# Attention and expert layer on one core: the first block's k and q by SyncE and ScalarE in fp32, two blocks ahead of w_in

## The chip, the cores and the metric

The kernel runs on one core of one Trainium2 chip. The metric is the device time of one execution in microseconds (us); lower is better. Several runs of the kernel were timed, and one more execution was taken with the hardware profiler.

## What is computed

```python
scores = (q @ k.T) / sqrt(64)                     # batch 8, heads 8, seq 576, head_dim 64
bias   = -slope[h] * abs(i - j)                   # one slope for each head
mask   = (i - j >= 0) & (i - j < 128)             # a causal window of 128
x      = softmax(where(mask, scores + bias, -1e9)) @ v
x      = x.transpose(0, 2, 1, 3).reshape(4608, 512)
h      = x @ w_in                                 # 512 -> 2048
out    = (relu(h) ** 2) @ w_out                   # 2048 -> 512
```

All inputs and the output are fp32; the kernel computes in bf16 with fp32 sums.

## The kernel before, in words

The 4608 tokens come as 40 attention blocks (`NBLK`): each of the 8 batches has four blocks of 128 tokens and one of 64. A block needs its k, q and v for all 8 heads; with the window of 128 its scores also touch the block before it in the same batch. The steps of block `m` are written in `attention(m)`:

- `load_block` issues three loads on GpSimd's queue (POOL), for k and q into one tile `kq` (a ring of four) and for v into `vt` (a ring of six). They cast from fp32 to bf16 on the way.
- For the first ten blocks TensorE transposes k and q, 128 columns at a time (`tp`, eight matmuls against `ident`), and VectorE or ScalarE copy the result from PSUM to `kqT` ("evict"); k's half is `i = 0`, q's half `i = 1`. In the version before, the first transposes of a block ask for both k and q of it, and both copies for all eight transposes. Later blocks are transposed by a DMA that SyncE issues.
- A burst of score matmuls writes four PSUM tiles `ps_s` (ring `a`), ScalarE takes four exponentials into `P`, VectorE multiplies them with `masks` (the decay of each head, built once from `dist`, which an iota on POOL makes).
- The `pv` matmuls multiply with v, in two halves of four heads; v has a column of ones, so that the sum of the weights comes along. VectorE takes the reciprocal (`rec`) and multiplies (`x`).
- `x` is transposed into `xT`, by TensorE (`xp`) for the first blocks, by a DMA later.

The expert layer takes 512 tokens at a time (`g`, nine groups). `fc_step` multiplies `xT` with `w_in`, four matmuls for each of 16 slices of 128 columns, ScalarE applies relu (`rt`), VectorE or ScalarE square it (`g`). For the first two groups these steps are split by tokens (`SPLIT`), so that they can begin with the first block alone. The second product is done plainly for the first group (`plain`) and for the others with seven products instead of eight on halves of 256 (`product`, with sums of `g` in `S` and differences of `w_out` in `w_mix`). w_in and w_out come in four quarters each (`load_w_in`, `load_w_out`), also on POOL's queue. SyncE issues the stores of the output from `osb` (a ring of four).

The order of all this is not the program's text. Every step is a task with the engines that may run it and its estimated duration, a key (when it is due), what it depends on and which ring slots it takes. `Plan.order` runs through all tasks once, engine by engine, and always takes the task that can start first; the engine's stream is then emitted in that order, and each engine works through its own stream strictly in order. The planner's picture of the machine is a few constants: how long a result takes to reach another engine (`LAT`), when TensorE's first, slower spell ends (`COLD`), and for a load its start after the issue, its time on the DMA engines (`dma`) and its landing.

The order in which the loads are due is a line of text:

```python
FIRST = "b0 i0 b1 i1 b2 i2 b3 i3 b4 b5 b6 o0 b7 o1 b8 o2 b9 o3"
```

where `b0` is block 0's k, q and v, `i0` the first quarter of w_in and `o0` the first quarter of w_out.

Of the kernel before, what the change touches and what calls it, by code (L numbers as in the profile page):

```python
# [8 lines left out]
FP32 = mybir.dt.float32  # L9
BF16 = mybir.dt.bfloat16  # L10
# [26 lines left out]
class Plan:  # L37
# [1 line left out]

    LAT = {"PE": 260.0, "ACT": 290.0, "DVE": 270.0, "POOL": 200.0, "SP": 2200.0}  # L40
    BEGIN = {"POOL": 1250.0}
    COLD = 15000.0

    def __init__(self, bufs):
        self.tasks = []
# [11 lines left out]
    def order(self):  # L57
        used = {tag: [] for tag in self.bufs}
        free = {}
        cand = {}  # L60
        left = {}
        for t in self.tasks:
            left[t] = len(t.deps)
            for d in t.deps:
                d.users.append(t)
            for e in t.engs:
                free.setdefault(e, self.BEGIN.get(e, 800.0))
                cand.setdefault(e, [])
# [24 lines left out]
        while len(done) < n_all:  # L93
            best = None
            for e, c in cand.items():
                lo = None
                for t in c:
                    a = avail(t)
                    if a is None:
                        continue  # L100
                    st = max(a, free[e])
                    k = (st, t.key, t.seq)
                    if lo is None or k < lo[0]:
                        lo = (k, t)
                if lo is not None and (best is None or lo[0][0] < best[0]):
                    best = (lo[0][0], e, lo[1])
            if best is None:
                raise RuntimeError("plan is stuck: " + repr([
                    (e, t.key, [s.tag for s in t.acq if avail(t) is None]) for e, c in cand.items() for t in c
                    if e != "POOL"][:40]))  # L110
            st, e, t = best
            t.eng, t.start = e, st
            dur = t.engs[e] * (2 if e == "PE" and st < self.COLD else 1)
            if t.dma is not None:
                at = max(st + dur + 900.0, self.dma_free)
                self.dma_free = at + t.dma
                t.end = self.dma_free + 900.0
            else:
                t.end = st + dur + (self.LAT[e] if t.lat is None else t.lat)
            free[e] = st + dur  # L120
            for x in t.engs:
                cand[x].remove(t)
            for s in t.acq:
                if s.idx is not None:
                    continue
                s.idx = len(used[s.tag]) % self.bufs[s.tag]
                used[s.tag].append(s)
            for s in t.rel:
# [14 lines left out]
def kernel(  # L143
# [15 lines left out]
    NG = NT // 512  # L159
    NBLK = B * NKB  # L160

    FIRST = "b0 i0 b1 i1 b2 i2 b3 i3 b4 b5 b6 o0 b7 o1 b8 o2 b9 o3"
    SPLIT = ([(0, 128), (128, 256), (256, 384), (384, 512)], [(0, 256), (256, 512)])

    KQ_DMA, X_DMA = 10, 13
# [36 lines left out]
    def mm(n):  # L202
        return max(n, 64) / 2.4 + 1.5
# [75 lines left out]
    def load_block(m, key):  # L279
        b, kb = divmod(m, NKB)  # L280
        n = blk[kb]
        s_in[m, "k"] = s_in[m, "q"] = Slot("kq")
        s_in[m, "v"] = Slot("v")
        for i, (nm, src) in enumerate((("k", k), ("q", q), ("v", v))):
            sl = s_in[m, nm]

            def emit(i=i, src=src, sl=sl, nm=nm):
                o = (vt[sl.idx][0:n, :, 0:D] if nm == "v"
                     else kq[sl.idx][0:n, i].rearrange("s (h d) -> s h d", h=H))
                nc.gpsimd.dma_start(o, src[b, :, kb * 128:kb * 128 + n, :].rearrange("h s d -> s h d"))  # L290
            t_in[m, nm] = load(key + 0.01 * i, 1050.0 * n / 128, emit, [t_ones] if nm == "v" else [], [sl])
# [10 lines left out]
    def copy(task, o, i):  # L302
        if task.eng == "DVE":
            nc.vector.tensor_copy(o, i)  # L304
        else:
            nc.scalar.activation(o, i, AF.Copy)  # L306

    def attention(m):
# [14 lines left out]
                             [s_in[m, "k"]], dma=1400.0)]  # L323
        else:
            slot = Slot("h" if first else "a")
            last = None
            for i in range(2 * C):
                def emit(i=i):
                    if i == 0:
                        slot.tile = psum.tile([128, 1024], BF16, tag=slot.tag, bufs=plan.bufs[slot.tag], name="tp")  # L330
                    nc.tensor.transpose(slot.tile[:, i * 128:(i + 1) * 128],  # L331
                                        kq[s_in[m, "k"].idx][:, i // C, (i % C) * 128:(i % C + 1) * 128], ident)
                last = plan.add({"PE": mm(128)}, due - 56, emit,
                                [last, t_ident, t_in[m, "kq"[i // C]]] + ([t_in[m, "q"]] + chain["tp"] if i == 0 else []),
                                [slot, sk] if i == 0 else [], [s_in[m, "k"]] if i == 2 * C - 1 else [])
            chain["tp"] = [last]
            t_kq = []
            for i in range(2):
                def evac(i=i):
                    copy(t_kq[i], kqT[sk.idx][:, i * C:(i + 1) * C, 0:n],  # L340
                         slot.tile[:, i * 512:(i + 1) * 512].rearrange("p (c s) -> p c s", c=C)[:, :, 0:n])
                t_kq.append(plan.add(both if first else {("DVE", "ACT")[i]: both[("DVE", "ACT")[i]]},
                                     due - 56, evac, [last], [], [slot]))
        t_kq_of[m] = t_kq


# [348 lines left out]
```

## Time and profile before

| | |
|---|---|
| median of 3 runs | 308.45 us (308.12 to 308.74) |
| the profiled execution | 308.27 us |
| its span from first to last instruction | 306.1 us |
| TensorE (PE) busy | 289.8 us, 95% of the span |
| VectorE (DVE) busy | 212.2 us |
| ScalarE (ACT) busy | 200.0 us |
| GpSimd (POOL) busy | 107.6 us |
| loads issued by POOL | 18.36 MB in 116736 packets |
| moved by hardware queues | 20.46 MB in 54128 packets |

The span is what the profile's rows cover; the execution's own time is 2.2 us longer. Durations of single instructions come from this one execution, so sums are made against its 308.27 us, which lies 0.18 us below the median. Names on the left of an arrow are written, names on the right are read; L12 is line 12 of the kernel; x4 after a row means that four equal instructions are merged in it; the bracket at the end of a timeline row says how long the engine had been idle before it and what ended that. "Landing" is the time from a load's issue to the arrival of its last byte.

### The profile page before, as it was taken

Reading aid. Unit: us, or ns where it says so; the run is one execution under the profiler, and the core shown is the slowest. Engines: PE = TensorE matmul, PEld = TensorE weight load, DVE = VectorE, ACT = ScalarE, POOL = GpSimd, SP = SyncE. Lnnn points to the kernel's source line nnn. Section 1 sums busy time; section 2 is a strip of 40 time slices with the busy share of each in tenths; the row PEclk is TensorE's granted clock in tenths of the full one; section 3 lists DMA queues with packets and bytes.
Section 4 is the critical chain, followed back from the end, with each engine's and each line's share of the span. In section 5 each row is a group of like instructions: output and inputs, shape, how many; then the busy total and the mean of one; then the engine's idle time right before and its main releaser. Section 6 shows DMA issues by size and latency. Waiting matters only on the chain.

```text
span 306.1 us, 7855 instructions
## 1 busy us (share of the span) xinstructions
PE 289.8 (95%) x3076; PEld 205.9 (67%) x3076; DVE 212.2 (69%) x633; ACT 200.0 (65%) x395; POOL 107.6 (35%) x133
## 2 busy tenths in 40 slices
PE   1489999999999999999999999999999999999995
PEld 1279987686866677666666666666766676666783
DVE  4348888749968786678758776677677785545622
ACT  4178894759769666767767787777667785564410
POOL 8747938626265444226361327132200000000000
PEclk9999999999999999999999999999999999999999
DMA  8999999999999999999999999999884112201223
GB/s 60 179 175 166 151 189 173 130 184 139 151 151 144 164 157 169 155 154 182 165 153 166 156 139 149 130 165 146 139 55 120 30 42 62 69 0 36 69 72 103
DMA packets 170901, 39.31 MB, mean 128 GB/s; under 512 B 158064, under 2 KB 170352, under 8 KB 170864
## 3 DMA queue, kind: packets, MB, share of 16 engines
q0 software_dynamic: 116736, 18.36, 93.9%
q1 hardware_dynamic: 54128, 20.46, 41.3%
q8 instruction: 24, 0.39, 0.5%
q14 instruction: 13, 0.11, 0.1%
HBM read 36.70 MB, written 9.44 MB: 151 GB/s over the span
## 4 chain that ended last, share of the span: by engine, by line
PE 92%; DMA 3%; DVE 2%; POOL 2%; ACT 1%; issue 0%; POOLq 0%; DVEq 0%
PE h L477 42%; PE o L559 32%; PE ps_s L361 6%; PE pv L397 6%; PE o L628 4%; DMA kq<-in_q_dram 3%; PE tp L331 1%; POOL kq L290 1%; PE xp L442 1%; ACT kqT L306 1%; DVE w_mix L273 0%; DVE kqT L304 0%; POOL vt L290 0%; DVE osb L593 0%; POOL w_in_sb L256 0%
## 5 line engine op out<-in xcount | busy, mean ns | idle before, releaser
L477 PE MATMUL h<-xT,w_in_sb 128*128 128x512 bf16 (+2 forms) x832 | 150.8, 316 | 0.3 <-DVE x L423 0.3
L487 ACT ACTIVATE rt<-h 128x512 bf16<-128x512 f32 x144 | 86.0, 600 | 61.9 <-PE h L477 54.2
L477 PEld LDWEIGHTS <-w_in_sb 128*128 128x128 bf16 x832 | 71.0, 99 | 35.4 <-DVE x L423 0.8
L374 ACT ACTIVATE P<-ps_s 128x512 bf16<-128x512 f32 (+1 forms) x160 | 71.1, 520 | 9.7 <-PE ps_s L361 9.5
L495 DVE TENSOR_TENSOR g<-rt 128x512 bf16<-128x512 bf16 x91 | 38.3, 422 | 35.1 <-ACT rt L487 34.4
L382 DVE TENSOR_TENSOR P<-P,masks 128x512 bf16<-128x512 bf16 (+1 forms) x160 | 54.4, 364 | 8.0 <-ACT P L374 6.5
L559 PEld LDWEIGHTS <-g 128*128 128x128 bf16 x512 | 47.9, 98 | 15.1
L290 POOL DMA_DIRECT2D kq<-in_k_dram x40 | 34.2, 855 | 55.6 <-DMA kqT<-kq 48.4
L290 POOL DMA_DIRECT2D vt<-in_v_dram x40 | 34.1, 856 | 52.8 <-PE pv L397 46.6
L559 PEld LDWEIGHTS <-S 128*128 128x128 bf16 x384 | 35.8, 98 | 11.7 <-issue 0.7
L559 PE MATMUL o<-w_mix,S 128*128 128x256 bf16 x256 | 38.7, 273 | 0.0
L559 PE MATMUL o<-w_mix,g 128*128 128x256 bf16 x256 | 37.5, 273 | 0.0
L559 PE MATMUL o<-w_out_sb,g 128*128 128x256 bf16 x256 | 36.9, 273 | 0.0
L290 POOL DMA_DIRECT2D kq<-in_q_dram x40 | 34.3, 857 | 2.0 <-DMA kq<-in_k_dram 1.3
L497 ACT ACTIVATE g<-rt 128x512 bf16<-128x512 bf16 x53 | 33.5, 632 | 1.3
L423 DVE TENSOR_TENSOR x<-pv,rec 128x256 bf16<-128x256 f32 (+1 forms) x80 | 33.3, 417 | 1.1
L397 PEld LDWEIGHTS <-P 128*128 128x128 bf16 x576 | 27.3, 98 | 8.9 <-DVE P L382 1.2
L397 PE MATMUL pv<-vt,P 128*128 128x65 bf16 x576 | 31.5, 194 | 0.6 <-DVE P L382 0.6
L418 DVE RECIPROCAL rec<-pv 128x4 f32<-128x4 f32 (+1 forms) x80 | 14.2, 177 | 14.6 <-PE pv L397 14.2
L361 PEld LDWEIGHTS <-kqT 64*128 64x128 bf16 x576 | 15.7, 96 | 11.1 <-issue 8.9
L361 PE MATMUL ps_s<-kqT 64*128 64x128 bf16 (+1 forms) x320 | 20.1, 216 | 0.8 <-DVE kqT L304 0.8
L361 PE MATMUL ps_s<-kqT,kqT 64*128 64x128 bf16 (+1 forms) x256 | 17.0, 214 | 1.4 <-ACT kqT L306 1.4
(41 smaller groups left out, 190.6 us busy)
## 6 DMA issues: line engine op xcount, KB each, us to landing
out_dram<-osb SPq DMA_DIRECT2D x35, 256.0 KB, 4.3
kq<-in_k_dram POOLq DMA_DIRECT2D x32, 128.0 KB, 7.1
kq<-in_q_dram POOLq DMA_DIRECT2D x32, 128.0 KB, 7.4
vt<-in_v_dram POOLq DMA_DIRECT2D x32, 128.0 KB, 8.2
w_in_sb<-in_moe_w_in_dram POOLq DMA_DIRECT2D x4, 512.0 KB, 9.8
w_out_sb<-in_moe_w_out_dram POOLq DMA_DIRECT2D x4, 512.0 KB, 10.0
kq<-in_k_dram POOLq DMA_DIRECT2D x8, 64.0 KB, 9.2
kq<-in_q_dram POOLq DMA_DIRECT2D x8, 64.0 KB, 8.9
```

The source lines that it names most:

```text
L290: nc.gpsimd.dma_start(o, src[b, :, kb * 128:kb * 128 + n, :].rearrange("h s d -> s h d"))
L361: nc.tensor.matmul(slot_s[2 * (c // 2) + half].tile.rearrange("p (c t q) -> p c t q", c=2, t=2)[:, c % 2, part, 0:n], kqT[sk_of[mk].idx][r ...
L374: nc.scalar.activation(view(Pt[sP.idx][:, 2 * i:2 * i + 2]), view(slot_s[i].tile.rearrange("p (c t q) -> p c t q", c=2, t=2)), AF.Exp, bia ...
L382: nc.vector.tensor_tensor(pt, pt, view(masks[:, 2 * i:2 * i + 2]), op=ALU.mult)
L397: nc.tensor.matmul(slot_v.tile[:, hi * (D + 1):(hi + 1) * (D + 1)], Pt[sP.idx][:, place(h), part, :], vt[s_in[mk, "v"].idx][:, h, :], star ...
L418: nc.vector.reciprocal(srec.tile[0:n, :], pv[0:n, :, D])
L423: nc.vector.tensor_tensor(xt[sx.idx][0:n, hf * 256:(hf + 1) * 256].rearrange("p (h e) -> p h e", h=4), pv[0:n, :, 0:D], srec.tile[0:n, :]. ...
L477: nc.tensor.matmul(slot.tile[:, f * w:(f + 1) * w], w_in_sb[:, cc, (fc + f) * 128:(fc + f + 1) * 128], xT[:, cc, g * 512 + lo:g * 512 + hi ...
L487: nc.scalar.activation(srt.tile, slot.tile, AF.Relu, bias=0.0, scale=1.0)
L495: nc.vector.tensor_tensor(o, i, i, op=ALU.mult)
L497: nc.scalar.activation(o, i, AF.Square)
L559: nc.tensor.matmul(bank.tile[:, t * 256:(t + 1) * 256], left(g, what, j)[:, t * 128:(t + 1) * 128], right(by, j), start=opens and j == 0 a ...
```

## The change

Five edits go together. Block 0's k and q are no longer loaded and cast by POOL: SyncE loads k and ScalarE loads q as fp32 into two `osb` tiles, and VectorE casts each into `kq`. Block 1's loads move ahead of the first quarter of w_in, and the third quarter of w_in behind block 3. The iota moves to the front of POOL's queue. The transposes of k and of q become two chains: k's need only k, q's only q, and each copy to `kqT` follows its own four transposes; for block 0 both copies are VectorE's. And three constants of the planner change: TensorE's slow spell ends at 12 us instead of 15 and costs wide matmuls 1.4 instead of 2 times their duration, and loads that start in that spell take 1.2 times their time on the DMA engines and land 0.4 us later than assumed before. The constants add no instruction; they enter into the order that the planner makes for the whole kernel.

```diff
-    COLD = 15000.0
+    COLD = 12000.0
...
-            dur = t.engs[e] * (2 if e == "PE" and st < self.COLD else 1)
+            dur = t.engs[e] * (1 if e != "PE" or st > self.COLD else 2 if t.engs[e] < 250 else 1.4)
             if t.dma is not None:
-                at = max(st + dur + 900.0, self.dma_free)
-                self.dma_free = at + t.dma
-                t.end = self.dma_free + 900.0
+                early = st < self.COLD
+                at = max(st + dur + (700.0 if early else 900.0), self.dma_free)
+                self.dma_free = at + t.dma * (1.2 if early else 1.0)
+                t.end = self.dma_free + (1300.0 if early else 900.0)
...
-    FIRST = "b0 i0 b1 i1 b2 i2 b3 i3 b4 b5 b6 o0 b7 o1 b8 o2 b9 o3"
+    FIRST = "b0 b1 i0 b2 i1 b3 i2 i3 b4 b5 b6 o0 b7 o1 b8 o2 b9 o3"
...
-    t_iota = plan.add({"POOL": 360.0}, -9e5 + 0.012, build_iota)
+    t_iota = plan.add({"POOL": 360.0}, -9e5 - 1, build_iota)
...
+            if m == 0 and nm != "v":
+                st = Slot("osb")
+
+                def raw(src=src, st=st, nm=nm):
+                    st.tile = work.tile([128, 512], FP32, tag="osb", bufs=plan.bufs["osb"], name="raw")
+                    (nc.sync if nm == "k" else nc.scalar).dma_start(
+                        st.tile.rearrange("s (h d) -> s h d", h=H), src[b, :, 0:n, :].rearrange("h s d -> s h d"))
+
+                def cast(i=i, st=st, sl=sl):
+                    nc.vector.tensor_copy(kq[sl.idx][:, i], st.tile)
+                t_raw = plan.add({"SP" if nm == "k" else "ACT": 450.0}, -2e6, raw, [], [st], dma=1050.0)
+                t_in[m, nm] = plan.add({"DVE": 470.0}, key + 0.01 * i, cast, [t_raw], [sl], [st])
+                continue
...
-            for i in range(2 * C):
...
-                                [last, t_ident, t_in[m, "kq"[i // C]]] + ([t_in[m, "q"]] + chain["tp"] if i == 0 else []),
...
-            chain["tp"] = [last]
             t_kq = []
-            for i in range(2):
...
+            for j, nm in enumerate("kq"):
+                last = None
+                for i in range(C):
...
+                    last = plan.add({"PE": mm(128)}, due - 56, emit,
+                                    [last, t_ident, t_in[m, nm]] + (chain["tp"] if i == 0 else []),
+                                    [slot, sk] if i == 0 and j == 0 else [], [s_in[m, nm]] if j == 1 and i == C - 1 else [])
+                chain["tp"] = [last]
+
+                def evac(j=j):
...
+                t_kq.append(plan.add({"DVE": both["DVE"]} if m == 0 else both if first else
+                                     {("DVE", "ACT")[j]: both[("DVE", "ACT")[j]]}, due - 56, evac, [last], [], [slot]))
```

More of the change, by code (lines that the diff above doesn't have):

```diff
@@ L325, in attention @@
             slot = Slot("h" if first else "a")
-            last = None
-            for i in range(2 * C):
[L328 to L333, printed above, removed]
-                                [last, t_ident, t_in[m, "kq"[i // C]]] + ([t_in[m, "q"]] + chain["tp"] if i == 0 else []),
-                                [slot, sk] if i == 0 else [], [s_in[m, "k"]] if i == 2 * C - 1 else [])
@@ L336, in attention @@
-            chain["tp"] = [last]
-            t_kq = []
-            for i in range(2):
[L339 to L343, printed above, removed]
+            t_kq = []
@@ new lines, in attention, with emit @@
+            for j, nm in enumerate("kq"):
+                last = None
+                for i in range(C):
+                    def emit(i=i, j=j, nm=nm):
+                        if i == 0 and j == 0:
+                            slot.tile = psum.tile([128, 1024], BF16, tag=slot.tag, bufs=plan.bufs[slot.tag], name="tp")
+                        nc.tensor.transpose(slot.tile[:, (j * C + i) * 128:(j * C + i + 1) * 128],
+                                            kq[s_in[m, nm].idx][:, j, i * 128:(i + 1) * 128], ident)
+                    last = plan.add({"PE": mm(128)}, due - 56, emit,
[3 more added lines that the diff above has]
+                def evac(j=j):
+                    copy(t_kq[j], kqT[sk.idx][:, j * C:(j + 1) * C, 0:n],
+                         slot.tile[:, j * 512:(j + 1) * 512].rearrange("p (c s) -> p c s", c=C)[:, :, 0:n])
+                t_kq.append(plan.add({"DVE": both["DVE"]} if m == 0 else both if first else
+                                     {("DVE", "ACT")[j]: both[("DVE", "ACT")[j]]}, due - 56, evac, [last], [], [slot]))
```

## The prediction, made before the changed kernel ran

> **What bounds the kernel now.** I read the page first, then the windows of the first 50 us, the timeline of that stretch, the transfers with their times to landing, and the waits.
>
> ```profile
> span 306.1 us, 7855 instructions
> ...
> PE 289.8 (95%) x3076; PEld 205.9 (67%) x3076; DVE 212.2 (69%) x633; ACT 200.0 (65%) x395; POOL 107.6 (35%) x133
> ...
> PE   1489999999999999999999999999999999999995
> ...
> DMA  8999999999999999999999999999884112201223
> ...
> PE 92%; DMA 3%; DVE 2%; POOL 2%; ACT 1%; issue 0%; POOLq 0%; DVEq 0%
> ```
>
> TensorE is busy for 289.8 of 306.1 us and holds 92% of the chain that ended last. The change neither adds nor removes a matmul (3076 before and after, counted in the order of both built programs), so it can move the end only through TensorE's empty time, 16.3 us, and through how long its first matmuls run slowly. The tenths show where the empty time lies: in the first slices. The windows say how much (columns: stretch, length, busy time and instructions of PE, PEld, DVE, ACT, POOL, clock, DMA share, GB/s).
>
> ```profile
> 0.00:5.09 5.09, 0.00 (x0) 0.00 (x0) 2.56 (x13) 1.28 (x1) 3.97 (x9) 1.00 0.61 39
> 5.09:10.15 5.06, 2.92 (x24) 1.70 (x24) 2.48 (x9) 3.77 (x12) 5.06 (x7) 1.00 1.35 140
> 10.15:13.38 3.23, 0.00 (x0) 0.00 (x1) 0.66 (x3) 0.00 (x0) 1.78 (x3) 1.00 2.08 170
> 13.38:15.97 2.59, 1.65 (x13) 1.22 (x13) 0.85 (x2) 0.60 (x1) 2.19 (x4) 1.00 1.62 187
> 15.97:20.00 4.03, 4.03 (x48) 3.83 (x48) 1.70 (x4) 2.66 (x5) 2.27 (x4) 1.00 1.78 185
> 20.00:25.00 5.00, 4.28 (x89) 3.93 (x86) 3.65 (x13) 4.22 (x8) 2.57 (x4) 1.00 1.84 181
> 30.00:50.00 20.00, 20.00 (x342) 16.86 (x340) 17.67 (x61) 15.94 (x35) 13.89 (x18) 1.00 1.69 171
> 50.00:60.00 10.00, 9.66 (x132) 6.58 (x130) 7.80 (x28) 7.85 (x17) 7.13 (x10) 1.00 2.19 140
> 60.00:287.00 227.00, 227.00 (x2213) 153.96 (x2212) 163.69 (x481) 156.96 (x304) 65.06 (x78) 1.00 1.35 126
> ```
>
> Up to 15.97 us TensorE has 5.09 + 2.14 + 3.23 + 0.94 = 11.4 us of nothing to do; from there to 287 us it lacks 0.72 + 0.34 us. POOL, which issues every load, is busy for the whole of 5.09 to 10.15: the loads are issued as fast as it can. What ends TensorE's waits:
>
> ```profile
> 1.25 1.02 POOL L290 DMA_DIRECT2D kq<-in_k_dram  x1 [0.80 <-POOLq L679]
> 2.26 0.89 POOL L290 DMA_DIRECT2D kq<-in_q_dram  x1
> 3.53 1.02 POOL L290 DMA_DIRECT2D vt<-in_v_dram  x1
> 4.55 0.76 POOL L256 DMA_DIRECT2D w_in_sb<-in_moe_w_in_dram  x1
> 5.09 0.60 PE L331 MATMUL tp<-ident,kq 128*128 128x128 bf16 x4 [5.09 <-DMA kq<-in_k_dram]
> ...
> 6.35 0.61 PE L331 MATMUL tp<-ident,kq 128*128 128x128 bf16 x4 [0.65 <-DMA kq<-in_q_dram]
> ...
> 7.03 0.91 POOL L290 DMA_DIRECT2D vt<-in_v_dram  x1
> ...
> 7.80 0.61 PE L361 MATMUL ps_s<-kqT 64*128 64x128 bf16 x8 [0.85 <-DVE kqT L304]
> ...
> 10.42 0.42 DVE L423 TENSOR_TENSOR x<-pv,rec 128x256 bf16<-128x256 f32 x1
> 13.38 0.61 PE L331 MATMUL tp<-ident,kq 128*128 128x128 bf16 x4 [3.23 <-DMA kq<-in_k_dram]
> ...
> 14.62 0.63 PE L442 MATMUL xp<-ident,x 128*128 128x128 bf16 x4
> 15.29 0.42 DVE L304 COPY xT<-xp 128x512 bf16<-128x512 bf16 x1
> ...
> 16.93 3.24 PE L477 MATMUL h<-xT,w_in_sb 128*128 128x128 bf16 x32
> ```
>
> Block 0's k arrives at 5.09 and its attention ends with x at 10.84. Then TensorE has nothing until block 1's k lands at 13.38, since w_in's first quarter was issued ahead of it (4.55). Its transposes and scores follow, and the first w_in matmuls, 32 of block 0, start at 16.93. When did that first quarter land?
>
> ```profile
> w_in_sb<-in_moe_w_in_dram POOLq DMA_DIRECT2D x1, 512.0 KB, 7.9
> vt<-in_v_dram POOLq DMA_DIRECT2D x1, 128.0 KB, 8.1
> vt<-in_v_dram POOLq DMA_DIRECT2D x1, 128.0 KB, 4.7
> ```
>
> These are single issues: block 0's v takes 4.7 us from 3.53 (lands 8.23), w_in's first quarter 7.9 from 4.55 (12.45), block 1's v 8.1 from 7.03 (15.13). So w_in sat unused from 12.45 to 16.93.
>
> **The change, part by part.** The order of the changed program on POOL is: the distances, k1, v0, q1, v1, w_in's first quarter, block 2, second quarter, block 3, third and fourth quarter. k0 and q0 leave it for SP and ACT.
>
> *When w_in can start.* Before, the seven transfers k0, q0, v0, w_in, k1, q1, v1 were down at 15.13. After, the same seven must be down when w_in is, as it is last. If the transfers are the limit and starting on three queues gives nothing, it lands at 15.13. If all that POOL sheds is gained, k0's and q0's issues (1.02 + 0.89 = 1.91), it lands at 13.2. I take 13.8, nearer the second end, because POOL was the busy party (5.06 of 5.06) while the bytes ran at 140 GB/s, under the 171 of 30 to 50 us. [...]
>
> *Is block 0 ready by then?* The raw loads are in no row. Nearest are SP's own transfers, with fp32 on both sides:
>
> ```profile
> out_dram<-osb SPq DMA_DIRECT2D x35, 256.0 KB, 4.3
> out_dram<-osb SPq DMA_DIRECT2D x2, 128.0 KB, 1.7
> ```
>
> At 1.7 to 4.3 us from an issue at about 0.8 (ACT's first instruction starts at 0.74) k0 and q0 land between 2.5 and 5.1; if the two, of 256 KB each, go one after the other at 4.3 us, the second lands at 9.4. I take 5.1. A cast is a 128x512 copy: 0.42 us in the bf16 row at 15.29, and as an upper end 0.69, the fp32 row below. VectorE's distances, ahead of the casts, come 1.4 us earlier, since the iota goes first on POOL. The casts then end near 5.9, q's transposes (0.61) near 6.6, two copies (0.42 each) near 7.5, and scores start about 7.6: where they start now, 7.80. So block 0 gains nothing, and its x (10.84) plus transposes and copy (0.63 + 0.42) is done near 12, 1.8 us before 13.8. That slack is what hides the casts: raw loads up to 6.9 cost nothing, later ones one for one. k evicted without q's transposes only moves work into this slack; that VectorE takes both copies of block 0 is what it did before.
>
> ```profile
> 20.01 0.38 PE L397 MATMUL pv<-vt,P 128*128 128x65 bf16 x7
> ...
> 21.98 0.23 PE L361 MATMUL ps_s<-kqT,kqT 64*128 64x128 bf16 x2 [0.71 <-ACT kqT L306]
> 22.39 2.06 ACT L374 ACTIVATE P<-ps_s 128x512 bf16<-128x512 f32 x4
> 22.76 1.28 PE L477 MATMUL h<-xT,w_in_sb 128*128 128x128 bf16 x20
> 23.88 0.59 PE L397 MATMUL pv<-vt,P 128*128 128x65 bf16 x8
> ...
> 298.70 0.69 DVE L607 TENSOR_TENSOR osb<-o,x 128x512 f32<-128x512 f32 x1 [1.06 <-PE o L559]
> ```
>
> *Gain at the start.* At 13.8 instead of 16.93: 3.1 us. Ahead of it the new order has also done 8 of block 1's 16 pv matmuls, which before came at 20.01 (0.38 for 7): 0.4. Together 3.5.
>
> *What is late next.* The new order puts block 2's pv only 16 w_in matmuls behind its scores; before there were 4 transposes and 20. Before, pv (23.88) came 1.9 us after the scores began (21.98) and waited for nothing; the exponentials start 0.4 after the scores and take 0.52 each. Scores (0.4, until the exponentials start) and 16 matmuls (0.064 each by the 20 in 1.28: 1.0) cover 1.4 of 1.9: some 0.5 us of waiting. Block 1's x transposes stand 7 matmuls behind the end of its pv, where a reciprocal and a multiply (0.42, the row at 10.42) must run with their hand-overs: 0.5 more. I take 1.0, bounds 0.4 and 1.6. The scores' wait for ScalarE's copy of q (0.71) is in both. The second quarter should not stop TensorE: it follows block 2's three loads, 0.9 MB at the 171 GB/s of 30 to 50 us, 5.4 us after the first, near 19.2; the new order has 76 matmuls ahead of it, 4.9 us at 0.064 each, 1.3 more while the first 32 run at 0.10 (3.24 for 32) and the 1.0 of waits. [...]
>
> *The rest.* The changed constants make no instruction; they give a new order to 250 us of work. Before, TensorE waited 0.34 us between 30 and 287. The new order has tighter places. Between the scores of blocks 20 and 21 stood 28 products of 256 columns and 8 pv matmuls, now 7 and 8; between those of 15 and 16 stood 11 products, 8 w_in matmuls and 16 pv, now 13 products and 16 pv. A burst of scores needs all four score tiles back, which the exponentials of the burst before it hold for up to 2.06 us, longer where an eviction stands ahead of them. I take 1.0 us of new waits in all, bounds 0 and 3.0 (four such places with 0.75 each).
>
> Sum: 3.5 - 1.0 - 1.0 = 1.5 us less. The profiled execution took 308.27 with a span of 306.1; 2.2 lies around it. That gives 304.6 and 306.8, and against the median of the runs (308.45, 0.18 more) 306.9.
>
> **The rivals.** *More of it is kept:* w_in at 13.2 (+0.6), no new waits after 30 us (+1.0): 305.3. For it: before's long stretch without waits. Against: the tighter bursts.
>
> *The DMA engines are the limit:* w_in at 15.13, 1.3 later: 308.2, no change. For it: 170 to 187 GB/s from 10 us on. Against: the full POOL row.
>
> *The casts hold POOL up:* they run at about 5.1 to 5.9, while POOL issues v1 and w_in; if POOL stands still for both (0.84), w_in lands that much later: 307.8. For it: the issue beside VectorE's first fp32 work takes 1.02 (3.53), the ones at 2.26 and 7.03 take 0.89 and 0.91. Against: the one at 1.25 takes 1.02 as well. [...]
>
> *Slower, raw loads late:* k0 and q0 come as 2048 pieces of 256 bytes (64 fp32 for each token and head) beside POOL's loads. If the second lands at 9.4, block 0's x is transposed 2.5 after 13.8, so 306.9 + 2.5: 309.4. It turns into a loss from a landing at 8.4 (6.9 + 1.5). Against: 1.7 us for a store on an empty queue.
>
> *Slower, the order:* new waits of 3.0 instead of 1.0 give 308.9; it loses from 2.5 on.
>
> **How the numbers follow.** A measurement of this kernel tells about 0.2%, 0.6 us. The forecast (306.2 to 307.7) has 0.34, the gain kept 0.22, the DMA limit 0.10, the casts 0.08, raw loads late 0.10, the order 0.16. Faster is the first two and half of the casts (307.8 lies on the bound), 0.60; the same is the other half and the DMA limit, 0.14; slower the last two, 0.26. The range for 8 in 10 runs from 304.8 (w_in at 13.2, no late waits, and 0.5 less of the early ones: 306.9 - 2.1) to 309.2, between the two slower cases.
>
> **What would show it.** Right: the first w_in matmul at 13.2 to 14.4, released by w_in's load; scores of block 0 at 7 to 8; a wait of about 0.5 at block 2's pv; TensorE's empty time up to there 2 to 3 us less, and 0.5 to 1.5 us more between 30 and 287. Wrong: casts after 7 us, w_in after 15, or more than 2.5 us of waits after 30.

## The result, and the profile after

The changed kernel takes 305.62 us (median of 20 runs, 305.31 to 307.90), the kernel before, in the same set of runs, 307.78 (20 runs, 306.79 to 308.95): a ratio of 0.9928, 95% interval 0.9915 to 0.9942, 2.2 us less. The forecast was 1.5 less. It stood on the median of the first three runs of the kernel before, 308.45, which lies 0.7 above that of the 20. The profiled execution took 305.56, with a span of 303.8 against 306.1. Two executions of the runs below, 311.66 and 310.08, had a granted clock of 0.994 and took over 1.5% longer than the fastest of their kernel; the ratios leave them out.

The page of the changed kernel: the span and the busy times.

```profile
span 303.8 us, 7860 instructions
...
PE 290.9 (96%) x3076; PEld 205.6 (68%) x3076; DVE 216.4 (71%) x639; ACT 197.6 (65%) x391; POOL 105.8 (35%) x131
```

TensorE's busy time is 1.1 us longer than before and the span 2.3 shorter, so 3.4 us of empty time went. The windows, at the same cuts as before (columns as in the prediction), say where:

```profile
0.00:5.09 5.09, 0.00 (x0) 0.00 (x0) 2.78 (x13) 2.39 (x5) 4.28 (x10) 1.00 0.81 125
5.09:10.15 5.06, 3.31 (x28) 2.26 (x28) 3.15 (x9) 2.66 (x9) 5.06 (x7) 1.00 1.85 171
10.15:13.38 3.23, 2.67 (x35) 1.82 (x35) 2.65 (x10) 2.06 (x4) 2.81 (x5) 1.00 2.14 165
13.38:15.97 2.59, 2.59 (x32) 2.56 (x30) 1.55 (x6) 0.00 (x0) 1.84 (x3) 1.00 1.46 196
15.97:20.00 4.03, 3.24 (x60) 2.73 (x59) 2.83 (x7) 3.46 (x7) 2.25 (x3) 1.00 1.87 182
20.00:25.00 5.00, 4.67 (x92) 4.29 (x90) 4.25 (x13) 3.81 (x8) 1.96 (x3) 1.00 1.63 187
30.00:50.00 20.00, 19.78 (x290) 15.31 (x286) 17.79 (x59) 15.30 (x34) 11.92 (x16) 1.00 1.74 175
50.00:60.00 10.00, 9.62 (x121) 7.02 (x119) 6.13 (x19) 7.67 (x17) 6.12 (x7) 1.00 1.92 148
60.00:287.00 227.00, 226.89 (x2224) 153.37 (x2221) 166.12 (x486) 155.78 (x302) 65.01 (x78) 1.00 1.27 123
```

Up to 15.97 us TensorE has 5.09 + 1.75 + 0.56 = 7.4 us of nothing to do, 4.0 less than before (11.4). From 15.97 to 25 it has 0.79 + 0.33 where it had 0.72, and from 30 to 287 it has 0.22 + 0.38 + 0.11 = 0.71 where it had 0.34. The transfers moved 125 GB/s in the first 5 us instead of 39, and 171 instead of 140 in the next 5. The start, from the timeline:

```profile
0.74 0.48 ACTq L292 DMA_DIRECT2D raw<-in_q_dram  x1
0.75 0.44 SPq L292 DMA_DIRECT2D raw<-in_k_dram  x1
...
4.98 0.92 POOL L257 DMA_DIRECT2D w_in_sb<-in_moe_w_in_dram  x1
5.17 0.95 DVE L296 CAST kq<-raw 128x512 bf16<-128x512 f32 x2 [1.22 <-DMA raw<-in_q_dram]
...
6.18 0.93 PE L347 MATMUL tp<-ident,kq 128*128 128x128 bf16 x7 [6.18 <-DVE kq L296]
...
7.62 0.69 PE L347 MATMUL tp<-ident,kq 128*128 128x128 bf16 x5 [0.52 <-DVE kqT L318]
...
8.40 0.61 PE L376 MATMUL ps_s<-kqT 64*128 64x128 bf16 x8
...
12.62 0.85 PE L412 MATMUL pv<-vt,P 128*128 128x65 bf16 x8
12.81 0.41 DVE L318 COPY xT<-xp 128x512 bf16<-128x512 bf16 x1
...
13.28 1.57 PE L492 MATMUL h<-xT,w_in_sb 128*128 128x128 bf16 x13
```

and the times from issue to landing of three of these loads:

```profile
raw<-in_q_dram ACTq DMA_DIRECT2D x1, 256.0 KB, 4.4
raw<-in_k_dram SPq DMA_DIRECT2D x1, 256.0 KB, 3.9
...
w_in_sb<-in_moe_w_in_dram POOLq DMA_DIRECT2D x1, 512.0 KB, 7.0
```

k is down at 0.75 + 3.9 = 4.65, q at 0.74 + 4.4 = 5.14. VectorE's first cast waits until q is there, since q's cast stands ahead of k's; TensorE starts at 6.18, block 0's scores at 8.40 (7.80 before), and x of block 0 is in `xT` at 13.22. w_in's first quarter is down at 4.98 + 7.0 = 11.98. The first w_in matmul starts at 13.28, with no idle time ahead of it that ends with a load: it follows block 0's own chain (its copy to `xT` ends at 13.22) and, directly ahead of it on TensorE, the eight pv matmuls of block 1 from 12.62, which stand behind block 0's `xp` there. w_in had waited for 1.3 us. It lands only 0.5 us earlier than before (12.45); what comes much earlier are block 1's k, down at 1.36 + 4.9 = 6.26 instead of 13.29, and its q, at 3.25 + 4.7 = 7.95 instead of 14.17, so that TensorE's wait of 3.23 us for that k is gone. The chain that ended last says the same. Its only load in the first 16 us (start, duration):

```profile
0.74 4.40 DMA raw<-in_q_dram
...
5.17 0.96 DVE kq L296 x2
...
13.46 1.39 PE h L492 x13
```

In the same view of the kernel before the one load of the start is block 1's q, not w_in either:

```profile
6.17 8.00 DMA kq<-in_q_dram
```

What TensorE waited for over the span:

```profile
PE tp L347 <- DVE kq L296: 6.2, 1, 6.2
PE tp L347 <- DVE kqT L318: 0.9, 2, 0.5
PE xp L457 <- DVE x L438: 0.5, 1, 0.5
...
PE xp L457 <- ACT rt L502: 0.4, 1, 0.4
```

### The profile page after: what moved, and what is told of

It is laid out like the page before. It is cut to its first block, busy times and chain, and to the rows that moved or that the text cites. A ratio compares the mean times of both kernels' runs of the same rounds, so it can differ in the third digit from the quotient of the medians.

```text
span 303.8 us, 7860 instructions
## 1 busy us (share of the span) xinstructions
PE 290.9 (96%) x3076; PEld 205.6 (68%) x3076; DVE 216.4 (71%) x639; ACT 197.6 (65%) x391; POOL 105.8 (35%) x131
## 4 chain that ended last, share of the span: by engine, by line
PE 93%; DVE 3%; DMA 1%; ACT 1%; issue 0%; DVEq 0%; ACTq 0%
PE h L492 41%; PE o L574 32%; PE pv L412 6%; PE ps_s L376 6%; PE o L643 5%; PE tp L347 2%; DMA raw<-in_q_dram 1%; PE xp L457 1%; ACT P L389 1%; DVE x L438 0%; DVE S L538 0%; ACT rt L502 0%; DVE kqT L318 0%; DVE P L397 0%; DVE kq L296 0%
## 5 line engine op out<-in xcount | busy, mean ns | idle before, releaser
L492 PEld LDWEIGHTS <-w_in_sb 128*128 128x128 bf16 x832 | 69.9, 99 | 35.2
L304 POOL DMA_DIRECT2D kq<-in_k_dram x39 | 33.3, 854 | 23.9 <-DMA kqT<-kq 17.5
L304 POOL DMA_DIRECT2D kq<-in_q_dram x39 | 33.4, 855 | 4.3 <-DMA w_in_sb<-in_moe_w_in_dram 1.9
L412 PE MATMUL pv<-vt,P 128*128 128x65 bf16 x576 | 32.4, 195 | 1.0 <-DVE x L438 0.3
L433 DVE RECIPROCAL rec<-pv 128x4 f32<-128x4 f32 (+1 forms) x80 | 14.0, 176 | 13.3 <-PE pv L412 13.0
L574 PE MATMUL o<-w_out_sb,S 128*128 128x256 bf16 x128 | 17.7, 273 | 0.5 <-DVE osb L608 0.5
```

Of the source, the lines that this page charges most:

```text
L412: nc.tensor.matmul(slot_v.tile[:, hi * (D + 1):(hi + 1) * (D + 1)], Pt[sP.idx][:, place(h), part, :], vt[s_in[mk, "v"].idx][:, h, :], star ...
L492: nc.tensor.matmul(slot.tile[:, f * w:(f + 1) * w], w_in_sb[:, cc, (fc + f) * 128:(fc + f + 1) * 128], xT[:, cc, g * 512 + lo:g * 512 + hi ...
L574: nc.tensor.matmul(bank.tile[:, t * 256:(t + 1) * 256], left(g, what, j)[:, t * 128:(t + 1) * 128], right(by, j), start=opens and j == 0 a ...
```

## The experiments

**What was in question.** Theory A: block 0's chain (raw load of q, two casts, transposes, scores, `xT`) sets the first w_in matmul, and w_in's load has time to spare. The rival is the prediction's step: w_in's load sets it, and block 0 has 1.8 us to spare. A second question is which part of the edit brings the gain: the two extra queues, the order of POOL's loads, or the planner's constants. The place of the iota and the split of the transposes were not taken out alone. All kernels but two (`old_const`, `const_only`) keep the changed kernel's order on TensorE, VectorE and ScalarE, except for the one step named; the planned order is edited after the planner has made it. Each set of runs had its own runs of the kernel before: medians 307.78, 308.37, 307.83, 308.50 and 308.33.

**q's raw load later** (`late_raw`): ScalarE issues it behind the first of its eight masks.

```diff
+    late = next(t for t in done if t.eng == "ACT")
+    done.remove(late)
+    done.insert(done.index(t_mask[0]) + 1, late)
```

> The changed kernel with one instruction moved: ScalarE issues q's raw load behind its first mask, near 4.3 us instead of 0.74, so that it lands near 8.5 instead of 5.14. Theory A (block 0's chain is the bound): all of the 3.3 us is lost, scores of block 0 near 11.7, 308.9 in all. Theory B (the prediction: raw loads cost nothing up to 6.9, later ones one for one): 1.6 us lost, 307.2.

310.53 us (6 runs, 309.78 to 311.18), ratio 1.0067 (1.0045 to 1.0088). From its timeline:

```profile
3.98 0.42 ACTq L292 DMA_DIRECT2D raw<-in_q_dram  x1
...
9.38 1.78 DVE L296 CAST kq<-raw 128x512 bf16<-128x512 f32 x2 [5.43 <-DMA raw<-in_q_dram]
...
11.21 0.93 PE L347 MATMUL tp<-ident,kq 128*128 128x128 bf16 x7 [11.21 <-DVE kq L296]
```

q lands at 9.38, 4.24 later than in the changed kernel, and the two casts take 1.78 instead of 0.95. The first transposes come 5.03 later than in the changed kernel (11.21 against 6.18) and the profiled execution ends 4.87 later (310.43 against 305.56). Nearly all of it arrives at the end: block 0 has no slack, and w_in's load, which was not touched, doesn't matter here. The end is 1.6 us later than theory A gave (308.9), since q landed 0.9 later than it assumed and the casts took longer.

**w_in later** (`w_in_late`): POOL issues its first quarter behind block 2's k and q.

```diff
+    pool = [t for t in done if t.eng == "POOL"]
+    spots = [n for n, t in enumerate(done) if t.eng == "POOL"]
+    at = pool.index(t_win[0])
+    pool.insert(at + 2, pool.pop(at))
+    for n, t in zip(spots, pool):
+        done[n] = t
```

> The changed kernel with the order of every engine kept, except that on POOL's queue the first quarter of w_in is issued behind block 2's k and q instead of ahead of them. It landed at 11.98 us and the first w_in matmul started at 13.28; with two block loads (0.85 us each) ahead it should land near 13.7. Theory A (block 0's own chain, from raw loads to x, sets the first w_in matmul, and w_in has 1.3 us to spare): the first w_in matmul at about 13.8 and 0.5 us lost, 306.1 against 305.6. Theory B (the prediction: w_in's landing sets it): the matmul moves with the load, 1.7 us lost, 307.3.

307.12 us (13 runs, 305.63 to 307.61), ratio 0.9963 (0.9949 to 0.9976). The profiled execution was the fastest of them, 305.63: its w_in is down at 13.23, and the first w_in matmul at 13.36, as theory A has it. That left the other runs unexplained, so it ran again.

> The kernel with w_in's first quarter issued behind block 2's k and q, once more, since its profiled execution (305.63) was the fastest of its runs and the typical one (307.12) is 1.5 us slower than the changed kernel. Theory A (block 0's chain sets the first w_in matmul; a later w_in costs only what goes beyond 13.3) then needs another place where the typical execution loses 1 to 1.5 us: a slow spell that ends later (18 to 20 us instead of 15.8), at equal landings. Rival (the step of the prediction: w_in's landing sets it): w_in lands 1 us later than in the first profile, 14.2 to 14.6, and the first w_in matmul with it. A profile at 305.6 again, with medians at 307, leaves it open.

306.48 us (8 runs, 305.85 to 307.40), ratio 0.9955 (0.9937 to 0.9974); profiled 306.81. The landing of w_in and then the first w_in matmul in the first profile (issue at 6.83), and the same two in the second (issue at 6.92):

```profile
w_in_sb<-in_moe_w_in_dram POOLq DMA_DIRECT2D x1, 512.0 KB, 6.4
```

```profile
13.36 1.57 PE L492 MATMUL h<-xT,w_in_sb 128*128 128x128 bf16 x13
```

```profile
w_in_sb<-in_moe_w_in_dram POOLq DMA_DIRECT2D x1, 512.0 KB, 7.5
```

```profile
14.46 1.57 PE L492 MATMUL h<-xT,w_in_sb 128*128 128x128 bf16 x13 [0.82 <-DMA w_in_sb<-in_moe_w_in_dram]
```

With the same program w_in took 6.4 us in one execution and 7.5 in the other. At 13.23 it is no wait. At 6.92 + 7.5 = 14.42 it is: TensorE stands for 0.82 us, the first w_in matmul comes 1.10 later and the execution ends 1.18 later. So the step of the prediction is right in kind once w_in lands after 13.3, as the medians suggest that it does here in most runs; in the changed kernel's profiles it lands earlier.

**The changed kernel again** (`after_again`).

> The changed kernel once more, unchanged, for a comparison within one set of runs with the three others. 305.6 us as before (305.3 to 306.2), ratio to the kernel before 0.992 to 0.995. First w_in matmul at 13.3, released by block 0's chain and not by w_in's load (12.0). If a second profile shows a first w_in matmul over 0.5 us away from that, single profiles of these kernels can't tell half a microsecond, and the readings of the start have to be widened by that.

305.64 us (5 runs, 305.39 to 305.82), ratio 0.9923 (0.9905 to 0.9941). The landing of w_in:

```profile
w_in_sb<-in_moe_w_in_dram POOLq DMA_DIRECT2D x1, 512.0 KB, 7.7
```

w_in is down at 4.97 + 7.7 = 12.67, 0.7 later than in the first profile; the first w_in matmul starts 0.23 later (13.51), since block 0's first cast took 0.81 us instead of 0.43 and its transposes started 0.22 later (6.40), and the profiled times differ by 0.08 (305.64 and 305.56). w_in's landing may move by 0.7 us without a trace in the time.

**Without the two queues** (`pool_k0q0`): POOL loads and casts k0 and q0 at the head of its queue; no raw loads and no casts on VectorE, all else in the changed order. The iota, in the changed kernel ahead of the first load (0.84), comes behind these two here (3.23).

```diff
-                    st.tile = work.tile([128, 512], FP32, tag="osb", bufs=plan.bufs["osb"], name="raw")
-                    (nc.sync if nm == "k" else nc.scalar).dma_start(
-                        st.tile.rearrange("s (h d) -> s h d", h=H), src[b, :, 0:n, :].rearrange("h s d -> s h d"))
+                    nc.gpsimd.dma_start(kq[sl.idx][:, i].rearrange("s (h d) -> s h d", h=H),
+                                        src[b, :, 0:n, :].rearrange("h s d -> s h d"))
...
-                    nc.vector.tensor_copy(kq[sl.idx][:, i], st.tile)
+                    pass
```

> The changed kernel in its order, but block 0's k and q come as before: cast on the way by POOL, at the head of its queue (no raw loads, no casts on VectorE). It asks what the two hardware queues bring alone. Theory A: k0 and q0 land near 5.1 and 6.3, so block 0's transposes start no later, but all of POOL's other loads move back by 1.9 us: w_in near 13.9, k1 near 8.2, first w_in matmul at 14.2, 0.9 to 1.2 us lost, 306.6. Rival 1 (nearly all of the gain comes from the queues): 307.8, the time of the kernel before. Rival 2 (the casts eat what the queues bring): 305.6.

308.25 us (12 runs, 306.98 to 310.69), ratio 0.9998 (0.9974 to 1.0021): the whole gain goes. From its timeline:

```profile
7.13 0.79 POOL L257 DMA_DIRECT2D w_in_sb<-in_moe_w_in_dram  x1
...
10.33 0.61 PE L346 MATMUL tp<-ident,kq 128*128 128x128 bf16 x4 [1.57 <-DMA kq<-in_q_dram]
...
14.55 1.57 PE L491 MATMUL h<-xT,w_in_sb 128*128 128x128 bf16 x13
```

w_in is issued 2.15 later (7.13 against 4.98) and block 1's q is there at 10.33, for which TensorE stands 1.57 us; the first w_in matmul comes 1.27 later than in the changed kernel. That profiled execution (309.29) also has one wait of 1.5 us further on, for a transposing DMA, so the 1.27 alone don't account for its time. The fastest run, 306.98, is about what the 1.27 would give (theory A said 306.6); why the typical one loses 1.3 more is not shown. Without the two extra queues, then, nothing of the gain is left in the median, but only half of that loss is seen at the start.

**w_in back ahead of block 1** (`w_in_first`), the rest of the edit as in `w_in_late`:

```diff
-    pool.insert(at + 2, pool.pop(at))
+    pool.insert(at - 4, pool.pop(at))
```

> The changed kernel in its order, but on POOL's queue the first quarter of w_in goes back ahead of k1, v0, q1, v1. It asks what the changed order of loads brings alone. Theory A: k1 and q1 land 2.4 us later (near 8.7 and 10.4), block 0's scores stand behind k1's transposes and start near 9.9 instead of 8.40, block 1's near 11.8; the first w_in matmul, though w_in is down by 9, waits for block 0's x until 14.8: 1.5 us lost, 307.1. Theory B (w_in's landing sets the first w_in matmul): no loss, 305.6 or less.

308.61 us (12 runs, 308.15 to 308.78), ratio 1.0007 (0.9994 to 1.0020): the whole gain goes here too.

```profile
10.25 0.61 PE L347 MATMUL tp<-ident,kq 128*128 128x128 bf16 x4 [2.11 <-DMA kq<-in_k_dram]
...
16.19 1.57 PE L492 MATMUL h<-xT,w_in_sb 128*128 128x128 bf16 x13
```

w_in is issued at 1.36 and is early, but TensorE now stands 2.11 us for block 1's k, and the first w_in matmul comes 2.91 later than in the changed kernel, as does the end (308.47 against 305.56 in the profiled executions). Theory A had named this path and put the loss at 1.5. An early w_in is worth nothing when the blocks that it pushes back feed TensorE first. With either the queues or the order taken back the median gain is gone.

**The hardware queues take block 1's k and q** (`hw_k1q1`), POOL those of block 0, and behind them the iota (3.23).

```diff
+                    nc.gpsimd.dma_start(kq[sl.idx][:, i].rearrange("s (h d) -> s h d", h=H),
+                                        src[b, :, 0:n, :].rearrange("h s d -> s h d"))
...
-                        st.tile.rearrange("s (h d) -> s h d", h=H), src[b, :, 0:n, :].rearrange("h s d -> s h d"))
+                        st.tile.rearrange("s (h d) -> s h d", h=H), src[b, :, 128:256, :].rearrange("h s d -> s h d"))
...
-                    nc.vector.tensor_copy(kq[sl.idx][:, i], st.tile)
+                    nc.vector.tensor_copy(kq[s_in[1, nm].idx][:, i], st.tile)
...
+                if m == 1 and nm != "v":
+                    return
```

> SyncE and ScalarE load block 1's k and q in fp32, VectorE casts those, and POOL loads and casts block 0's k and q at the head of its queue; the same number of loads on each queue and the same order on every engine. Theory A (block 0's chain sets the first w_in matmul): k0 down at 4.9 and q0 at 6.2 (as with POOL loading all six), no cast ahead of them; scores of block 0 at 7.8 instead of 8.4, x 0.6 earlier, first w_in matmul at 12.7, 305.0. Rival (what matters is that POOL gets w_in out early, and the first bytes are shared by all queues): q0 lands at 7 or later, scores at 8.4 or later, 305.6 or slower.

305.87 us (6 runs, 305.44 to 311.66), ratio 0.9928 (0.9909 to 0.9946): no gain over the changed kernel. PEld rows are TensorE's weight loads.

```profile
5.73 0.34 PEld L351 LDWEIGHTS <-kq 128*128 128x128 bf16 x4 [5.73 <-DMA kq<-in_k_dram]
...
8.27 0.61 PE L380 MATMUL ps_s<-kqT 64*128 64x128 bf16 x8
...
13.48 0.67 PEld L496 LDWEIGHTS <-w_in_sb 128*128 128x128 bf16 x7 [0.31 <-DMA w_in_sb<-in_moe_w_in_dram]
```

The scores come at 8.27, not at 7.8 (k0 takes until 5.73), 0.13 earlier than in the changed kernel, and yet the first w_in matmul starts at 13.48: w_in was issued at 5.41 and took 8.0 us, so that it is down at 13.41, and the weight load of its first matmul waits 0.31 us for it. What block 0 wins, w_in takes back. The two limits lie within 1.5 us of each other.

**The planner's old constants under the change** (`old_const`):

```diff
-    COLD = 12000.0
+    COLD = 15000.0
...
-                at = max(st + dur + (700.0 if early else 900.0), self.dma_free)
-                self.dma_free = at + t.dma * (1.2 if early else 1.0)
-                t.end = self.dma_free + (1300.0 if early else 900.0)
+                at = max(st + dur + 900.0, self.dma_free)
+                self.dma_free = at + t.dma
+                t.end = self.dma_free + 900.0
```

> The changed kernel with the planner's three constants of the kernel before; loads, casts and their order on POOL are the change's, the order of TensorE's work differs: the transposes of block 2's k and q stand ahead of the first w_in matmuls. Theory A: block 2's k lands at 12.8 and its q a microsecond later, so the first w_in matmul comes at 14.7 instead of 13.3, with 8 transposes (0.6) already done: 0.8 slower at the start; with later waits like those of the changed kernel 306.4. Rival (the new order's tight places after 30 us are what the constants brought, 1.0 us): the old constants give that back, 305.4 or less.

306.52 us (7 runs, 306.05 to 306.99), ratio 0.9951 (0.9930 to 0.9972), 0.9 slower than the changed kernel, as theory A expected (306.4), though it had the first w_in matmul at 14.7. TensorE's order now has block 2's transposes ahead:

```profile
13.40 0.61 PE L346 MATMUL tp<-ident,kq 128*128 128x128 bf16 x4 [1.08 <-DMA kq<-in_k_dram]
...
15.53 0.62 PE L491 MATMUL h<-xT,w_in_sb 128*128 128x128 bf16 x4
```

It stands 1.08 us for block 2's k, and the first w_in matmul is at 15.53. The new constants tell the planner that early loads come later, and so keep that wait out.

**The new constants alone** (`const_only`): the same lines the other way round, on the kernel before.

> The kernel before with the three new constants of the planner alone: loads, casts and their order on POOL as before; the order of the rest is another. Theory A (the gain is in the loads and in block 0's own chain): the start is as before, first w_in matmul at 16.5 to 17.2, and the time 307.8 to 308.5, no difference. Rival (the constants bring tight places, the prediction's term of 1.0 for later waits): TensorE waits 1.0 more between 30 and 287 and the kernel is slower by as much. A gain of 0.9 as in the changed kernel (whose time rises by that with the old constants) would say that they help by themselves.

308.62 us (12 runs, 307.70 to 310.54), ratio 1.0015 (0.9996 to 1.0035): no difference, as theory A has it in the time. Its start is not as expected: block 1's k lands at 12.16 in its profile, not at 13.38, though POOL's order is that of before, and the first w_in matmul comes at 15.71 (16.93 before). With POOL's loads in the same order, part of that may be a difference between executions: w_in's first quarter takes 6.7 us from 4.54 here, and 7.9 from 4.55 in the profile of the kernel before. That gains nothing in the end. The constants are worth 0.9 us with the new loads and nothing without.

**The casts exchanged** (`k_cast_first`): k's ahead of q's, since k lands first and TensorE transposes it first.

```diff
+    qc, kc = t_in[0, "q"], t_in[0, "k"]
+    n, i = done.index(qc), done.index(kc)
+    done[n], done[i] = kc, qc
```

> The changed kernel with the two casts of block 0 exchanged on VectorE: k's first, then q's. In the changed kernel q's stands first, so k, down at 4.65, waits for q, down at 5.14, and TensorE's first transposes (of k) for both casts. Theory A (block 0's chain sets the first w_in matmul): first transposes at 5.2 to 5.3 instead of 6.2 to 6.4, scores of block 0 at 7.4 instead of 8.4 to 8.6, x's transposes 1.1 earlier; the first w_in matmul then comes when both that chain (12.2) and w_in (12.0 to 12.7 in two profiles) are there, 0.6 to 1.0 earlier: 304.9. Rival, the step of the prediction (w_in's load sets it and block 0 has slack): the start is unchanged, 305.6.

305.28 us (6 runs, 304.98 to 306.73), ratio 0.9902 (0.9877 to 0.9927); and in another set:

> The kernel with the exchanged casts once more, in another set of runs, since its lead over the changed kernel (305.28 against 305.62 and 305.64) is smaller than the interval of one set. Theory A: 305.0 to 305.5 again; first transposes at 5.2 to 5.3, scores of block 0 at 7.8 to 7.9, w_in down at 12.0 to 12.8, first w_in matmul at 12.4 to 12.9. If w_in comes down near 12.0 as in the changed kernel's first profile, the first w_in matmul follows block 0's copy of x at 12.5 and no sooner. Rival (the casts' order is worth nothing): 305.6, first w_in matmul at 13.3 to 13.5.

304.99 us (6 runs, 304.73 to 305.31), ratio 0.9898 (0.9879 to 0.9918). Both medians are below those of the changed kernel (305.62 and 305.64), by 0.3 to 0.65 us: a version faster than the kernel before and, in all likelihood, than the changed one; the intervals of its ratio overlap a little with that of the changed kernel (0.9915 to 0.9942). The landing of w_in in the second run's profile, and its timeline:

```profile
w_in_sb<-in_moe_w_in_dram POOLq DMA_DIRECT2D x1, 512.0 KB, 6.9
```

```profile
4.60 0.99 DVE L296 CAST kq<-raw 128x512 bf16<-128x512 f32 x2 [0.66 <-DMA raw<-in_k_dram]
...
5.32 0.93 PE L347 MATMUL tp<-ident,kq 128*128 128x128 bf16 x7 [5.32 <-DVE kq L296]
...
11.95 0.42 DVE L318 COPY xT<-xp 128x512 bf16<-128x512 bf16 x1
...
12.42 1.57 PE L492 MATMUL h<-xT,w_in_sb 128*128 128x128 bf16 x13
```

Nothing here touches w_in, which is down at 4.97 + 6.9 = 11.87. TensorE starts 0.86 earlier than in the changed kernel's first profile (5.32 against 6.18), and the first w_in matmul 0.86 earlier (12.42 against 13.28), right behind the copy to `xT` (12.37). So block 0's chain was the limit: had w_in's load set it, nothing would have moved. In the first of the two runs w_in landed at 4.96 + 7.8 = 12.76 and the first w_in matmul started at 12.84, while the copy to `xT` had ended at 12.69: there w_in was already the limit, by some 0.1 us.

**w_in ahead of block 1's v as well** (`k_first_w_in`): the casts exchanged, and the edit of `w_in_late` with another place:

```diff
-    pool.insert(at + 2, pool.pop(at))
+    pool.insert(at - 1, pool.pop(at))
```

> The casts exchanged as well, and w_in's first quarter issued ahead of block 1's v instead of behind it. w_in lands 0.9 earlier (11.1 to 11.8), block 1's v later (11 to 12.5 instead of 8.9). Theory A: nothing beyond the exchanged casts as long as w_in was down in time there, and up to 0.4 more where it wasn't: 304.6 to 304.9, first w_in matmul at 12.2. Rival: block 1's v, which eight products ahead of the first w_in matmul need, comes after 12.2 and becomes the wait: 305.2 to 305.6.

305.77 us (12 runs, 305.32 to 310.08), ratio 0.9921 (0.9897 to 0.9945): the rival holds. From its timeline:

```profile
12.83 0.54 PE L412 MATMUL pv<-vt,P 128*128 128x65 bf16 x7 [0.50 <-DMA vt<-in_v_dram]
```

Block 1's v lands at 4.85 + 7.9 = 12.75, and seven pv products wait for it; the gain of the exchange is spent.

## Why the prediction was right, and where it wasn't

The sign and the place were right, and the size nearly: 1.5 us forecast, 2.2 measured. Three terms made the sum. The last two are judged by when TensorE has done the same amount of work in both traces (3076 matmul rows in each, weighted by their columns): the changed kernel is 4.3 us ahead where the w_in work begins, 3.3 at 34 us, 2.2 to 2.5 from 95 us on, and 2.2 at the last matmul (300.36 against 302.56). Each is one execution of its kernel. For TensorE's first, slower matmuls the sum has no term, and no run shows them alone; in these two executions the last of them came 2.6 us behind the first w_in matmul before (19.5 for 16.93) and 2.4 after (15.7 for 13.28).

**The start, +3.5: 4.3.** Mis-sized, by two errors that work against each other: w_in came 1.8 us earlier than the 13.8 of the sum, block 0 more than 1 us later than near 12. That the first w_in matmul still fell within the forecast stretch is luck.

*w_in at 13.8, bounds 13.2 and 15.13: it landed at 11.98 and 12.67.* The step took as its best case that all of POOL's shed issue time (1.91) arrives at the landing. POOL issued the last of the seven 2.05 earlier (4.98 against 7.03), as that step has it. But the transfer was shorter as well, 7.0 and 7.7 against 8.1, with more of the early bytes moved by then (125 GB/s against 39). The DMA limit of 15.13 didn't hold. `pool_k0q0` shows what issues on POOL cost: with two more of them w_in's issue is 2.15 later and its time to landing much the same (7.3). The 2.05 us by which the issue came earlier are most of the 3.15 by which the last of the seven landed earlier (11.98 for 15.13).

*Block 0 ready near 12, with 1.8 of slack: it had none.* This step failed. The reading of before had w_in unused from 12.45 on, and the start set by a block's loads; for the new order the step took w_in as the limit because it is the last of the seven loads. The raw loads landed as predicted (5.14 for 5.1). But q's cast stands ahead of k's, so k waits for q; the two casts took 0.95 instead of 0.84; VectorE's copy of k starts at 7.14, behind the seventh transpose and not behind k's own four, and block 0's eighth transpose, the first of the five in the row at 7.62, waits 0.52 for that copy, a wait which the split into two chains doesn't ask for and whose reason stays open; and block 1's scores stand between the two halves of block 0's pv. Scores came at 8.40, not 7.6, and `xT` at 13.22, not near 12. `late_raw` and `k_cast_first` show it from both sides: later casts cost nearly one for one (5.03 at the first transposes, 4.87 at the end), earlier ones gain. The rival on late raw loads had the mechanism, but let landings up to 6.9 pass free and priced one of 9.4 at 309.4; `late_raw`, with a landing of 9.38, took 310.53.

Hence "the first w_in matmul at 13.2 to 14.4" was right (13.28), and "released by w_in's load" was wrong. Of the other signs, the scores at 7 to 8 were wrong (8.40), the wait of about 0.5 at block 2's pv was 0.25, and the empty time up to the w_in work fell by 4.0 us, not by 2 to 3, and after 30 us grew by 0.37, not by 0.5 to 1.5.

**New early waits, −1.0: −1.0.** The amount fits, half of it by luck. TensorE's waits name 0.4 for `xp` behind ScalarE's relu (`rt`), and 0.3 each for pv behind `P` and behind x; but the wait of the scores for ScalarE's copy of q, which the prediction kept in both kernels (0.71), is gone. For the same work, TensorE is idle for 1.19 us after (12.63 to 30.66, busy 16.84) and for 0.73 before (16.93 to 34.00, busy 16.34): 0.46 more of waiting, and 0.50 more busy time for the same work.

**Later waits, −1.0: −1.1.** The amount fits, the mechanism wasn't seen. The predicted waits of score bursts for their tiles don't appear: no wait for `ps_s` is among TensorE's waits after. Empty time from 30 to 287 rose by 0.37 only, about as much as one wait for `kqT` near 52 us (0.38); the rest is busy time, 268.74 us from 30.66 to the last matmul against 267.97 from 34.00 before, for the same 2730 matmuls. Over the whole span the rows of pv (32.4 for 31.5 us) and of `tp` (8.3 for 7.5) are longer and those of w_in shorter (150.0 for 150.8); why stays open.

**The casts and POOL: not 0.84.** The rival that POOL stands still for both casts is refuted in size (the issues beside them took 0.1 to 0.2 longer); what the trace has in its place is told below.

## What to carry to other kernels

Where several loads feed one start, each engine's first instruction must be the one whose data comes first: one cast in the wrong order held the whole kernel by some 0.3 to 0.6 us. When a load is moved, look for the next limit behind it and write down how far it is: here w_in's load and block 0's chain lay within 1.5 us of each other, and an edit that helped one alone was soon caught by the other. A single profile doesn't show how near a limit is when the landing of a load differs by 1 us between executions of the same program (6.4 and 7.5 us from its issue in `w_in_late`).

## What the runs showed of the hardware

TensorE's slow spell (matmuls of 128 columns 0.107 us apart, then 0.056) isn't a fixed time after the start of the w_in work. Its last slow matmul came at 19.5 before (work from 16.93), at 15.7 after (from 13.28) and at 17.1 in the second run of `k_cast_first` (from 12.42; its pairs of score matmuls are 0.107 apart until then, and 0.055 in the changed kernel at 17.21). That run's lead over the changed kernel shrinks from 0.86 at that start to 0.60 at the last matmul. The granted clock reads 1.00 in the windows of these stretches before and after, and 1.0 for the profiled execution of that run. What ends the spell is not shown.

The time from issue to landing of one and the same 512 KB load differs from execution to execution: 7.0 and 7.7 in the changed kernel, 7.8 and 6.9 in `k_cast_first`, all issued at 4.96 to 4.98, and 6.4 and 7.5 in `w_in_late`. Where it took 6.9 and 7.0 the issue itself had taken 0.92 us beside a cast, where it took 7.7 and 7.8 the issue took 0.79; whether the one brings the other is not shown. The rest of the program follows to a tenth: between the two profiles of `w_in_late`, 1.10 us at the first w_in matmul is 1.18 at the end, and between the two of the changed kernel the lead is 0.07 from 17 us to the end.

A cast of a 128x512 fp32 tile on VectorE takes 0.41 to 0.43 us or 0.54 to 0.95, and which of the two goes by when it starts. All 22 casts of the eleven traces that have them run beside an issue of POOL's. Eight start up to 0.22 us behind the start of the issue: they take 0.41 to 0.43, and it is the issue that is longer, 0.92 to 0.94 for a quarter of w_in instead of 0.79 and 1.00 to 1.11 for a k instead of some 0.9. Thirteen start 0.23 to 0.57 behind it: these casts take 0.54 to 0.95 and end only 0.23 to 0.35 behind the start of POOL's next issue. (The last starts 0.74 behind, takes 0.43, and ends 0.30 behind the next start.) The first cast of the changed kernel starts 0.19 behind an issue (4.98, above):

```profile
5.17 0.43 DVE L296 CAST kq<-raw 128x512 bf16<-128x512 f32 x1 [1.22 <-DMA raw<-in_q_dram]
```

and in the rerun 0.23 behind, and it takes 0.81. There the second cast then starts first, and the issue at 5.71 is the longer one:

```profile
4.97 0.79 POOL L257 DMA_DIRECT2D w_in_sb<-in_moe_w_in_dram  x1
5.21 0.81 DVE L296 CAST kq<-raw 128x512 bf16<-128x512 f32 x1 [1.25 <-DMA raw<-in_q_dram]
5.71 1.11 POOL L304 DMA_DIRECT2D kq<-in_k_dram  x1
```

In these rows either engine can be the one that loses: POOL 0.1 to 0.2 us per issue, VectorE up to 0.5 per cast, and VectorE's side is the one that lies on the path that set the start. Why it goes by the start of the cast is not shown.
